# A decode layer on one core: w_gate loaded in two parts, residual sums moved between their matmuls, a smaller last load, and the store on another queue

## The chip, the cores and the metric

One core of a Trainium2 chip runs the kernel. The metric is the device time in microseconds (us) of one execution. A profile adds the kernel's *span*, which is 1.7 to 1.8 us shorter than the time that is measured from outside. Engines: PE is TensorE (PEld its weight loads), DVE is VectorE, ACT is ScalarE, SP is SyncE. SBUF is the on-chip memory that the loads fill, PSUM the one that TensorE writes its sums to.

## The reference

One token passes through an attention block and a gated MLP, batch 1, all in bf16:

```
x: [1, 1, 640]
h  = x + attention(layernorm(x))      # 32 heads, 4096 cached keys and values of 128 each, wq [640, 4096], wo [4096, 640]
g  = layernorm(h) @ w_gate            # [640, 1728]
u  = layernorm(h) @ w_up              # [640, 1728]
h2 = h + (gelu(g) * u) @ w_down       # [1728, 640]
```

Every weight and every cached row is used once. The bytes that must be read (84.2 MB; the kernel reads 84.3, since one load fetches rows that are already there) are therefore fixed, and the arithmetic on them is small.

## The kernel before

All big loads are issued by SyncE on one queue, in the order in which they are needed: wq, keys and values in turn, wo, and then the three MLP matrices. Three slots of SBUF hold keys, values and finally the MLP weights. The part that the change touches is the end. There hlnT is layernorm(h) as TensorE's operand, hX holds h for the residual sum, and hm is gelu(g) * u:

```python
    # issue order on SyncE, behind the last values and wo
    d_wd = [P.dma("sync", wd_sb[:, 12, :], B_w_down[1536:1664, :], free[1]),
            P.dma("sync", wd_sb[:, 13, :], B_w_down[1600:1728, :])]      # only its partitions 64 to 127 are used
    d_wg = P.dma("sync", wg_sb, B_w_gate[:, :].rearrange("(p c) n -> p c n", c=5), free[0])
    d_wu = [P.dma("sync", wu_sb[:, 0:3, :], wu_v[:, 0:3, :]),
            P.dma("sync", wu_sb[:, 3:5, :], wu_v[:, 3:5, :])]
    d_wd += [P.dma("sync", wd_d[:, 0:2, :, :], wd_v[:, 0:2, :, :]),      # "the bulk", 8 rows per partition
             P.dma("sync", wd_d[:, 2, 0:2, :], wd_v[:, 2, 0:2, :]),      # 2 rows
             P.dma("sync", wd_d[:, 2, 2:4, :], wd_v[:, 2, 2:4, :])]      # 2 rows, the last load
    # ...
    ga = T(glu(ps_g, wg_sb, range(5)), hl, d_wg)      # 70 matmuls: layernorm(h) @ w_gate
    T(resid, hx)                                      # residual sum: h into the output's PSUM
    T(glu(ps_u, wu_sb, range(3)), d_wu[0])            # 42 matmuls: w_up
    up = T(glu(ps_u, wu_sb, range(3, 5)), d_wu[1])    # 28
    # ... gelu(g) on DVE and ACT, then hm = gelu(g) * u
    T(down([12, 13], False), g9, d_wd[0], d_wd[1])    # 4 matmuls for each m
    T(down(range(8), False), d_wd[2])
    T(down([8, 9], False), d_wd[3])
    dn = T(down([10, 11], True), d_wd[4])
    # four copies PSUM -> out_row, two on DVE, two on ACT
    d_out = P.dma("sync", out[0, :, :], out_row[:, :], *os)
    P.op("sync", None, d_out)                         # wait for the store
```

The softmax here doesn't subtract the row's maximum and nothing guards it: scores larger than these inputs give would overflow.

Of the kernel before, what the change touches and what calls it, by code (L numbers as in the profile page):

```python
# [92 lines left out]
def bass_sequential_preLN__gqa_block_cached__glu_gated_geglu__decode_kernel(nc, A_x, A_k_cache, A_v_cache, A_wq, A_wo, B_x, B_w_gate, B_w_up, B_w_down, out):  # L93
# [11 lines left out]
    out_row = sb("out_row", [1, D], BF16)  # L105
# [29 lines left out]
    ps_g, ps_u = bank[0], bank[1]  # L135
# [11 lines left out]
    P = Prog(nc)  # L147
    V = lambda fn, *d: P.op("vector", fn, *d)
    A = lambda fn, *d: P.op("scalar", fn, *d)
    T = lambda fn, *d: P.op("tensor", fn, *d)  # L150
# [66 lines left out]
    def layernorm(src, ev, out_fn):  # L217
        s2 = V(lambda e: e.tensor_mul(src[:, 5:10], src[:, 0:5], src[:, 0:5]), ev)
        m = T(lambda e: e.matmul(ps_s[:, 16:26], mean_f[:, :], src[:, 0:10], start=True, stop=True), s2, c_mean)
        l1 = V(lambda e: e.reduce_sum(ln[:, 0:2], ps_s[:, 16:26].rearrange("p (a c) -> p a c", a=2), axis=AX.X), m)  # L220
        l2 = V(lambda e: e.scalar_tensor_tensor(out=ln[:, 2:3], in0=ln[:, 0:1], scalar=ln[:, 0:1],  # L221
                                                in1=ln[:, 1:2], op0=ALU.mult, op1=ALU.subtract), l1)
        l3 = A(lambda e: e.activation(ln[:, 3:4], ln[:, 2:3], ACTF.Ln, bias=eps_t[:, 0:1], scale=-1.0), l2, c_eps)  # L223
        l4 = A(lambda e: e.activation(ln[:, 4:5], ln[:, 3:4], ACTF.Exp, bias=zero_t[:, 0:1], scale=-0.5), l3)
        return V(out_fn, l4)
# [117 lines left out]
    for G in range(NG):  # L343
# [6 lines left out]
        if G == 4:  # L350
# [11 lines left out]
    free = [consumed[len(order) - NSLOT + i] for i in range(1, 3)]  # L362
    wg_sb = sl[0][:, 0:5 * DF].rearrange("p (c n) -> p c n", c=5)
# [3 lines left out]
    wd_v = B_w_down[0:1536, :].rearrange("(a p r) n -> p a r n", a=3, r=4)  # L367
    wd_d = wd_sb[:, 0:12, :].rearrange("p (a r) n -> p a r n", a=3)
    d_wd = [P.dma("sync", wd_sb[:, 12, :], B_w_down[1536:1664, :], free[1]),
            P.dma("sync", wd_sb[:, 13, :], B_w_down[1600:1728, :])]  # L370
    d_wg = P.dma("sync", wg_sb, B_w_gate[:, :].rearrange("(p c) n -> p c n", c=5), free[0])
    d_wu = [P.dma("sync", wu_sb[:, 0:3, :], wu_v[:, 0:3, :]),
            P.dma("sync", wu_sb[:, 3:5, :], wu_v[:, 3:5, :])]
    d_wd += [P.dma("sync", wd_d[:, 0:2, :, :], wd_v[:, 0:2, :, :]),
             P.dma("sync", wd_d[:, 2, 0:2, :], wd_v[:, 2, 0:2, :]),
             P.dma("sync", wd_d[:, 2, 2:4, :], wd_v[:, 2, 2:4, :])]

    V(lambda e: e.memset(ps_g[0:64, 13:14], 0.0), reds[31])
    V(lambda e: e.memset(ps_u[0:64, 13:14], 0.0), reds[31])
# [4 lines left out]
    hl = layernorm(hT, h, lambda e: e.tensor_scalar(  # L384
        hlnT[:, :], hT[:, 0:5], ln[:, 0:1], ln[:, 4:5], ALU.subtract, ALU.mult))
# [4 lines left out]
    def glu(ps, w, cs):  # L390
        def fn(e):
            for c in cs:
                for m in range(14):
                    ws = w[:, c, 512 * (m // 4) + m % 4:512 * (m // 4) + 512:4] if m < 12 else \
                        w[:, c, 128 * m:min(128 * m + 128, DF)]
                    i = e.matmul(ps[0 if m < 13 else 64:128, m:m + 1], ws, hlnT[:, c:c + 1],  # L396
                                 start=(c == 0 and m == 0), stop=(c == 4), skip_group_check=True)
            return i
        return fn
    ga = T(glu(ps_g, wg_sb, range(5)), hl, d_wg)  # L400


    def resid(e):
# [2 lines left out]
                         hX[:, 32 * q:32 * q + 32, :].rearrange("p a c -> p (a c)"), start=True, stop=False)  # L406
        return i
    T(resid, hx)
    T(glu(ps_u, wu_sb, range(3)), d_wu[0])
    up = T(glu(ps_u, wu_sb, range(3, 5)), d_wu[1])  # L410
    g1 = V(lambda e: e.tensor_copy(g_t[:, :], ps_g[:, 0:14]), ga)
# [9 lines left out]
    def down(ms, last):  # L421
        def fn(e):
            for m in ms:
                k = slice(0 if m < 13 else 64, 128)
                for q in range(4):
                    i = e.matmul(ps_d[32 * q:32 * q + 1, 0:160], hm[k, m:m + 1], wd_sb[k, m, 160 * q:160 * q + 160],  # L426
                                 start=False, stop=(last and m == ms[-1]))
            return i
        return fn
    T(down([12, 13], False), g9, d_wd[0], d_wd[1])  # L430
    T(down(range(8), False), d_wd[2])
    T(down([8, 9], False), d_wd[3])
    dn = T(down([10, 11], True), d_wd[4])
    os = [V(lambda e, q=q: e.tensor_copy(out_row[0:1, 160 * q:160 * q + 160], ps_d[32 * q:32 * q + 1, 0:160]), dn)  # L434
          for q in range(2)]
    os += [A(lambda e, q=q: e.copy(out_row[0:1, 160 * q:160 * q + 160], ps_d[32 * q:32 * q + 1, 0:160]), dn)
           for q in range(2, 4)]
    d_out = P.dma("sync", out[0, :, :], out_row[:, :], *os)
    P.op("sync", None, d_out)

    with nc.Block() as block:  # L441
        P.emit(block)
# [28 lines left out]
```

## Time and profile before

| | before |
|---|---|
| time, median of 3 runs | 205.82 us (205.62 to 205.85) |
| span of the profiled run | 204.0 us |
| SyncE's load queue, share of the 16 DMA engines' span | 97.0% |
| mean rate | 414 GB/s |
| last landing of a load | 201.30 us |
| from the last landing to the end of the span | 2.74 us |

Part 3 of the page of the kernel before, with packets, MB and the share of 16 engines' span for each DMA queue:

```profile
q1 hardware_dynamic: 4306, 84.32, 97.0%
q8 instruction: 8, 0.13, 0.3%
q14 instruction: 3, 0.02, 0.0%
q10 hardware_dynamic: 2, 0.00, 0.0%
```

The load queue is busy nearly all the time. The first thing to establish is therefore whether a change reaches the length of this stream, or the short piece behind it. On this reading nothing else can move the end.

The timeline of the kernel before, its last stage: start, duration, engine, line, operation, out<-in, count, and in brackets the idle time before it and what ended it. Lines that the argument doesn't need are left out, here and below.

```profile
191.54 3.35 PE L396 MATMUL bank<-hlnT,slot 128*128 128x1 bf16 x70 [3.22 <-DMA slot<-in_B_w_gate_dram]
195.48 3.38 PE L396 MATMUL bank<-hlnT,slot 128*128 128x1 bf16 x70
198.96 0.17 DVE L419 TENSOR_TENSOR hm<-gu,bank 128x14 bf16<-128x14 f32 x1 [2.20 <-PE bank L396]
199.19 0.32 PEld L426 LDWEIGHTS bank<-slot,hm 128*1 128x1 bf16 x8 [0.42 <-DVE hm L419]
199.78 1.16 PEld L426 LDWEIGHTS bank<-slot,hm 128*1 128x1 bf16 x40 [0.28 <-DMA slot<-in_B_w_down_dram]
201.34 0.10 PEld L426 LDWEIGHTS bank<-slot,hm 128*1 128x1 bf16 x8 [0.40 <-DMA slot<-in_B_w_down_dram]
201.83 0.60 ACT L436 CAST out_row<-bank 1x160 bf16<-1x160 f32 x2 [5.75 <-PE bank L426]
201.83 0.66 DVE L434 CAST out_row<-bank 1x160 bf16<-1x160 f32 x2 [2.70 <-PE bank L426]
202.52 0.32 SPq L51 DMA_DIRECT2D out_dram<-out_row  x1
```

Gate's 70 matmuls wait 3.22 us for their load. w_up's 70 have no wait: they run behind gate and the residual sum. hm is ready at 199.13 (198.96 + 0.17), and from there TensorE waits twice more for w_down: 0.28 us for the bulk and 0.40 us for the last load. Everything after 201.34 stands behind the last landing.

One row of the table of stretches of the kernel before (stretch, its length, busy time and count of PE, PEld, DVE, ACT and POOL, granted clock, DMA share, GB/s) shows the clock that TensorE has in this stage:

```profile
195.50:198.80 3.30, 3.30 (x74) 3.14 (x70) 0.79 (x5) 0.31 (x1) 0.00 (x0) 0.50 0.96 383
```

So TensorE is slow here, with a granted clock of 0.50, and busy all through the stretch. It still has to wait for the loads afterwards.

### The profile page before, as it was taken

To read this page: it belongs to the slowest core of one execution; us is meant where nothing else is said; L and a number is where in the kernel's file an instruction comes from. 1 tells how busy PE (TensorE), PEld (TensorE's weight loads), DVE (VectorE), ACT (ScalarE), POOL (GpSimd) and SP (SyncE) were. 2 spreads that over 40 slices of the span, in tenths; PEclk is the share of its full clock that TensorE was granted. 3 is DMA by queue.
4 is the path that set the end of the run, shared out by engine and by line. 5 is a ranking of instruction groups with operands and counts; after the bars stand their busy time and mean duration, and the time that the engine had idled before them with its cause. 6 is when DMAs were issued, how large, how long until landed. Compare 5 with 4: busy or idle time off the path is not lost.

```text
span 204.0 us, 2507 instructions
## 1 busy us (share of the span) xinstructions
PE 121.1 (59%) x1009; PEld 58.9 (29%) x1009; DVE 100.9 (49%) x104; ACT 61.1 (30%) x273; POOL 4.1 (2%) x12
## 2 busy tenths in 40 slices
PE   1007049567667808690977297637834787467494
PEld 1003013122222503250324032312411244267482
DVE  3100187799279327924791677287608760101221
ACT  2100103626706610670156035503630363100101
POOL 8000000000000000000000000000000000000000
PEclk9999757978969975998599859988995899965555
DMA  7999999999999999999999999999999999999991
GB/s 249 434 442 411 411 488 430 418 411 442 430 430 424 418 427 463 424 419 418 443 450 424 421 424 438 443 430 418 424 434 450 389 440 435 413 409 425 415 393 55
DMA packets 4319, 84.47 MB, mean 414 GB/s; under 512 B 466, under 2 KB 724, under 8 KB 1492
## 3 DMA queue, kind: packets, MB, share of 16 engines
q1 hardware_dynamic: 4306, 84.32, 97.0%
q8 instruction: 8, 0.13, 0.3%
q14 instruction: 3, 0.02, 0.0%
q10 hardware_dynamic: 2, 0.00, 0.0%
HBM read 84.31 MB, written 0.00 MB: 413 GB/s over the span
## 4 chain that ended last, share of the span: by engine, by line
DMA 64%; PE 14%; DVE 14%; SPq 4%; issue 3%; DVEq 0%
DMA slot<-in_A_k_cache_dram 43%; DVE prod L252 12%; DMA slot<-in_A_v_cache_dram 11%; DMA slot<-in_B_w_down_dram 10%; PE bank L260 10%; SPq L51 4%; PE bank L289 3%; DVE sc L267 2%; PE bank L298 1%; PE bank L426 0%; DVEq L441 0%; DVE out_row L434 0%; PE bank L309 0%; DVE RT L308 0%
## 5 line engine op out<-in xcount | busy, mean ns | idle before, releaser
L260 PE MATMUL bank<-prod,id_b 128*128 128x512 bf16 x256 | 75.8, 457 | 53.6 <-DVE prod L252 53.5
L252 DVE TENSOR_TENSOR prod<-slot,qb 128x4096 bf16<-128x4096 bf16 x32 | 72.4, 2284 | 31.6 <-DMA slot<-in_A_k_cache_dram 31.6
L271 ACT ACTIVATE p_bd<-sc,zero_t 32x32 bf16<-32x32 f32 x128 | 46.4, 363 | 89.0 <-DVE sc L267 87.8
L260 PEld LDWEIGHTS bank<-prod,id_b 128*128 128x128 bf16 x256 | 27.1, 114 | 102.5 <-DVE prod L252 66.1
L267 DVE TENSOR_REDUCE sc<-bank 128x32 f32<-128x512 f32 x32 | 22.0, 688 | 21.5 <-PE bank L260 21.4
L271 ACT ACTIVATION_READ_ACCUMULATOR p_bd<-sc,zero_t 32x1 f32 x128 | 23.5, 184 | 0.0
L289 PE MATMUL bank<-slot,p_bd 128*16 128x512 bf16 x256 | 17.2, 379 | 0.6 <-DMA slot<-in_A_v_cache_dram 0.6
L289 PEld LDWEIGHTS bank<-slot,p_bd 128*16 128x16 bf16 x256 | 9.4, 89 | 4.8 <-DMA slot<-in_A_v_cache_dram 1.1
L238 PE MATMUL bank<-arena,xlnB 128*32 128x512 bf16 x40 | 4.1, 586 | 11.3 <-DMA arena<-in_A_wq_dram 11.3
L298 PE MATMUL bank<-po_sb,hs 128*16 128x128 f32 x64 | 8.4, 274 | 1.1 <-ACT po_sb L293 1.1
L327 PE MATMUL bank<-aP,arena 128*128 128x1 bf16 x160 | 6.7, 178 | 3.8 <-DMA arena<-in_A_wo_dram 3.8
L396 PE MATMUL bank<-hlnT,slot 128*128 128x1 bf16 (+1 forms) x140 | 6.7, 176 | 3.2 <-DMA slot<-in_B_w_gate_dram 3.2
L327 PEld LDWEIGHTS bank<-aP,arena 128*128 128x128 bf16 x160 | 6.6, 131 | 4.0 <-DMA arena<-in_A_wo_dram 2.6
L396 PEld LDWEIGHTS bank<-hlnT,slot 128*128 128x128 bf16 (+1 forms) x140 | 6.3, 118 | 4.1 <-issue 3.8
L242 DVE CAST qb<-bank 128x512 bf16<-128x512 f32 x1 | 0.7, 692 | 13.8 <-PE bank L238 13.8
L293 ACT COPY po_sb<-bank 128x512 f32<-128x512 f32 x8 | 4.7, 586 | 7.6 <-PE bank L289 7.6
L298 PEld LDWEIGHTS bank<-po_sb,hs 128*16 128x16 f32 x64 | 5.5, 96 | 4.5 <-issue 2.1
L223 ACT ACTIVATE ln<-ln,eps_t 128x1 f32<-128x1 f32 x2 | 0.6, 294 | 17.0 <-DVE ln L221 17.0
L238 PEld LDWEIGHTS bank<-arena,xlnB 128*32 128x32 bf16 x40 | 1.6, 141 | 13.3 <-issue 13.3
L383 DVE TENSOR_TENSOR hT<-xx,bank 128x5 f32<-128x5 f32 x1 | 0.2, 161 | 10.3 <-PE bank L327 10.3
L243 ACT CAST qb<-bank 128x512 bf16<-128x512 f32 x1 | 0.6, 586 | 14.3 <-PE bank L238 14.3
L313 DVE TENSOR_SCALAR aT<-bank,rz 16x128 bf16<-16x128 f32 x2 | 0.7, 339 | 6.0 <-PE bank L298 6.0
(59 smaller groups left out, 24.6 us busy)
## 6 DMA issues: line engine op xcount, KB each, us to landing
slot<-in_A_k_cache_dram SPq DMA_DIRECT2D x8, 4096.0 KB, 22.3
slot<-in_A_v_cache_dram SPq DMA_DIRECT2D x7, 4096.0 KB, 17.4
arena<-in_A_wq_dram SPq DMA_DIRECT2D x1, 5120.0 KB, 15.4
slot<-in_A_v_cache_dram SPq DMA_DIRECT2D x2, 2048.0 KB, 20.9
arena<-in_A_wo_dram SPq DMA_DIRECT2D x1, 2560.0 KB, 28.7
slot<-in_B_w_gate_dram SPq DMA_DIRECT2D x1, 2160.0 KB, 15.4
arena<-in_A_wo_dram SPq DMA_DIRECT2D x1, 1920.0 KB, 32.8
slot<-in_B_w_up_dram SPq DMA_DIRECT2D x1, 1296.0 KB, 18.0
```

Source lines behind the costliest of these rows:

```text
L51: ev = self.op(eng, lambda e: e.dma_start(out, in_), *deps, dma=True)
L238: i = e.matmul(ps_q[hf][32 * j:32 * j + 32, :], xlnB[:, c, :], wq_j[:, c, j, 4 * hf:4 * hf + 4, :], start=(c == 0), stop=(c == 4))
L242: qa = V(lambda e: e.tensor_copy(qb[:, 0:4, :].rearrange("p g d -> p (g d)"), ps_q[0][:, :]), qd)
L252: m = V(lambda e: e.tensor_tensor(out=prod[:, s % 4, :, :], in0=kt[:, 32 * u:32 * u + 32, :], in1=qb[:, G, :].unsqueeze(1).to_broadcast([1 ...
L260: i = e.matmul(ps_f[s % 2][:, :], id_b[:, :], prod[:, s % 4, :, 16 * b:16 * b + 16], start=(b == 0), stop=(b == 7))
L267: reds[s] = V(lambda e: e.reduce_sum(sc[:, s % 4, :], ps_f[s % 2][:, :].rearrange("p (g d) -> p g d", d=16), axis=AX.X), folds[s], exps.ge ...
L271: x = A(lambda e, j=j: e.activation(p_bd[32 * j:32 * j + 32, G % 2, 32 * (s % 4):32 * (s % 4) + 32, j], sc[32 * j:32 * j + 32, s % 4, :], ...
L289: i = e.matmul(po[a:a + 16, :], p_bd[:, G % 2, 4 * b:4 * b + 4, :].rearrange("p g j -> p (g j)"), vt[:, 4 * b:4 * b + 4, :], start=(b < 4) ...
L293: evs[G] = A(lambda e: e.copy(po_sb[:, G % 2, :], po[:, :]), pvs[G], hds.get(G - 2))
L298: i = e.matmul(ps_a[0:16, 128 * (G // 4):128 * (G // 4) + 128], hs[:, r, 12 - 4 * g:28 - 4 * g], po_sb[:, G % 2, 128 * r:128 * r + 128], s ...
L327: r = e.matmul(ps_p[:, c:c + 1], wo_sb[:, t, i, c::5], aP[:, t, i:i + 1], start=(t == 0 and c == 0 and i == 0), stop=(t == 1 and i == 15), ...
L396: i = e.matmul(ps[0 if m < 13 else 64:128, m:m + 1], ws, hlnT[:, c:c + 1], start=(c == 0 and m == 0), stop=(c == 4), skip_group_check=True)
```

## The change

Its intent: let gate start as soon as three fifths of w_gate are there; use the wait for the rest for the residual sums; leave as little work as possible behind the last load; and take the store to the queue of the engine that does the last copies.

```diff
-    d_wg = P.dma("sync", wg_sb, B_w_gate[:, :].rearrange("(p c) n -> p c n", c=5), free[0])
+    wg_v = B_w_gate[:, :].rearrange("(p c) n -> p c n", c=5)
+    d_wg = [P.dma("sync", wg_sb[:, 0:3, :], wg_v[:, 0:3, :], free[0]),
+            P.dma("sync", wg_sb[:, 3:5, :], wg_v[:, 3:5, :])]
     ...
-             P.dma("sync", wd_d[:, 2, 0:2, :], wd_v[:, 2, 0:2, :]),
-             P.dma("sync", wd_d[:, 2, 2:4, :], wd_v[:, 2, 2:4, :])]
+             P.dma("sync", wd_d[:, 2, 0:3, :], wd_v[:, 2, 0:3, :]),
+             P.dma("sync", wd_d[:, 2, 3:4, :], wd_v[:, 2, 3:4, :])]
     ...
-    ga = T(glu(ps_g, wg_sb, range(5)), hl, d_wg)
+    T(glu(ps_g, wg_sb, range(3)), hl, d_wg[0])
     ...
     T(resid, hx)
+    ga = T(glu(ps_g, wg_sb, range(3, 5)), d_wg[1])
     ...
-    T(down([8, 9], False), d_wd[3])
-    dn = T(down([10, 11], True), d_wd[4])
+    T(down([8, 9, 10], False), d_wd[3])
+    dn = T(down([11], True), d_wd[4])
     ...
-    d_out = P.dma("sync", out[0, :, :], out_row[:, :], *os)
-    P.op("sync", None, d_out)
+    d_out = P.dma("scalar", out[0, :, :], out_row[:, :], *os)
+    P.op("scalar", None, d_out)
```

## The prediction

> **What bounds the kernel.** The loads on SyncE's DMA queue. The table of DMA queues gives that queue 97.0% of the 16 engines' span, at a mean of 414 GB/s; the slices show DMA at nine tenths from the second to the next to last. The chain of waits is 64% DMA and ends: last w_down load (landing at 201.30), last matmul group 0.47, copies 0.66, the store, end at 204.0. TensorE is not the limit in the last stage, although the table of stretches grants it a clock of 0.5: hm is ready at 199.13, the first eight w_down matmuls start at 199.19, the next wait 0.28 for the load landing at 199.74, and the last eight 0.40 for the load landing at 201.30. So only the 2.7 us after the last landing, and the stream's length, can move the time.
>
> **The change, part by part.**
>
> 1. *w_gate in two loads.* Three fifths would land some 2 us (864 KB at about 413 GB/s) before 191.41, at about 189.3, so the first 42 gate matmuls can start when hlnT is ready (189.76), not at 191.54. Gate should end near 193.9 with the residual sums between, instead of 194.9. w_up's landings (194.50, 196.62) then gate w_up: hm ready near 198.2 instead of 199.13. But w_down's bulk lands at 199.74 whatever TensorE does. Slack grows (0.28 to about 1.3 us); the end doesn't move.
> 2. *Residual sums between* (0.71 us of TensorE): moved in slack, nothing.
> 3. *Stream.* Same bytes. w_gate's packets of 17280 B took 644 ns; they become 10368 and 6912 B, which w_up's already are, at 389 and 263 ns: 8 ns more for each of eight rows per engine, 0.06 us. The w_down tail, two 2560 B packets at 102 ns, becomes 3840 B (about 150, estimated) and 1280 B at 55: nothing. Last landing: +0 to +0.1 us.
> 4. *Last load halved.* Four matmuls after the last landing instead of eight. The second group of four starts only 0.09 us after the first, so 0.09 us is saved. The load before it lands 0.4 us later (about 200.9, was 200.51); its 12 matmuls take under 0.4 us, so just fit ahead of 201.3. At worst they delay the last four by 0.1.
> 5. *Store by ScalarE's queue.* The copies end at 202.49 and SyncE's issue starts at 202.52: no dead hop to remove. The issue took 0.32 us and landed 0.8 after it. ScalarE's only DMA issue (x, at the start) took 0.51 us, SyncE's first 0.38. [...] Expect -0.05 to +0.2 us.
>
> Sum: +0.06 - 0.09 + 0.05, nearly nothing. **Predicted 205.7 us, 8 in 10 between 204.9 and 206.4; faster by over 2%: 0.01, within 2%: 0.98, slower: 0.01.**
>
> **What would show it.** In the timeline after: gate starts near 189.8, hm ready about 1 us earlier; a longer wait of w_down's matmuls for the 199.7 landing; last landing within 0.3 us of 201.3; the last matmuls about 0.09 us shorter; the store issued by ScalarE for at least 0.3 us right after 202.4. DMA share and GB/s as before.
>
> **What would make it wrong.** A stream at another rate (1% is 2 us) from the other packet sizes; issues that block SyncE longer (two took 1.40 and 3.32 us) with one more load queued; a store clearly slower or faster from ScalarE; or the 12 matmuls running into the last four.

The sum: +0.06 - 0.09 + 0.05 = +0.02 us.

## The result, and the profile after

The kernel after takes 205.55 us (median of 5 runs, 205.35 to 205.84). The kernel before takes 205.62 us over its 5 runs (205.38 to 205.85). The ratio is 0.9997, with a 95% interval of 0.9984 to 1.0011: the same.

The DMA queues of the kernel after (packets, MB, share):

```profile
q1 hardware_dynamic: 4448, 84.31, 97.1%
q8 instruction: 8, 0.13, 0.3%
```

There are 142 packets more, and the bytes and the share are as good as unchanged (84.31 MB against 84.32, 97.1% against 97.0%). The timeline of the kernel after, same stage and columns as before:

```profile
189.72 2.06 PE L398 MATMUL bank<-hlnT,slot 128*128 128x1 bf16 x42 [1.50 <-DVE hlnT L386]
191.70 0.71 PE L407 MATMUL bank<-hX,ones_f 128*1 128x160 f32 x8
192.35 1.38 PE L398 MATMUL bank<-hlnT,slot 128*128 128x1 bf16 x28
194.48 3.49 PE L398 MATMUL bank<-hlnT,slot 128*128 128x1 bf16 x70 [0.75 <-DMA slot<-in_B_w_up_dram]
198.07 0.17 DVE L422 TENSOR_TENSOR hm<-gu,bank 128x14 bf16<-128x14 f32 x1 [2.48 <-PE bank L398]
198.30 0.32 PEld L429 LDWEIGHTS bank<-slot,hm 128*1 128x1 bf16 x8 [0.42 <-DVE hm L422]
199.70 0.89 PEld L429 LDWEIGHTS bank<-slot,hm 128*1 128x1 bf16 x32 [1.09 <-DMA slot<-in_B_w_down_dram]
200.87 0.23 PEld L429 LDWEIGHTS bank<-slot,hm 128*1 128x1 bf16 x12 [0.28 <-DMA slot<-in_B_w_down_dram]
201.27 0.09 PEld L429 LDWEIGHTS bank<-slot,hm 128*1 128x1 bf16 x4 [0.17 <-DMA slot<-in_B_w_down_dram]
201.63 0.59 ACT L439 CAST out_row<-bank 1x160 bf16<-1x160 f32 x2 [6.72 <-PE bank L429]
201.63 0.66 DVE L437 CAST out_row<-bank 1x160 bf16<-1x160 f32 x2 [3.38 <-PE bank L429]
202.32 0.23 ACTq L51 DMA_DIRECT2D out_dram<-out_row  x1
```

Gate now starts 1.8 us earlier (189.72 against 191.54), and what ends its wait is hlnT, not the load. hm is ready at 198.24 instead of 199.13. That gain turns into waits at once: 0.75 us for w_up where there was none, and 1.09 us for the bulk of w_down where there was 0.28. The matmuls of the bulk start at 199.70 instead of 199.78. Behind the last landing (201.23) the first copy starts after 0.40 us instead of 0.53, and the span ends after 2.60 us instead of 2.74.

### The profile page after: what moved, and what is told of

It reads as the page before. It is cut to its first block, busy times and chain, and to the rows that moved or that the text cites. A ratio compares the mean times of both kernels' runs of the same rounds, so it can differ in the third digit from the quotient of the medians.

```text
span 203.8 us, 2508 instructions
## 1 busy us (share of the span) xinstructions
PE 120.8 (59%) x1009; PEld 58.7 (29%) x1009; DVE 100.8 (49%) x104; ACT 61.1 (30%) x273; POOL 4.1 (2%) x12
## 3 DMA queue, kind: packets, MB, share of 16 engines
q1 hardware_dynamic: 4448, 84.31, 97.1%
HBM read 84.31 MB, written 0.00 MB: 414 GB/s over the span
## 4 chain that ended last, share of the span: by engine, by line
DMA 65%; PE 15%; DVE 15%; issue 2%; SPq 2%; DVEq 0%
DMA slot<-in_A_k_cache_dram 44%; DVE prod L252 12%; DMA slot<-in_A_v_cache_dram 11%; DMA slot<-in_B_w_down_dram 11%; PE bank L260 9%; PE bank L289 3%; DVE sc L267 2%; SPq L51 2%; PE bank L298 1%; PE bank L429 1%; DVEq L444 0%; DVE out_row L437 0%; PE bank L309 0%; DVE RT L308 0%
```

## The experiments

**The theories.** A: the end is set by the last landing of the load stream and by what follows it; the gate part only makes slack on TensorE; the end gains about 0.1 us from the smaller last load. B: TensorE at half clock does lie on the path, and another part of the change ate what gate gained. C: one of the parts of the tail alone made the whole gain of the tail. D: the gate part made no slack that can be used at all.

Three columns of the table below come from the landing records of each profile. Each of these loads runs on 16 DMA engines, and each engine reports its part: there are 16 reports for a load. *Mean landing* and *last landing* are taken over the 16 reports of the last load. *Tail* is the span minus the last landing. The experiments ran in three groups, each on one chip together with the kernel before: e1, e3, e4 and e5 (before 205.60 us, median of 11 runs), e2, e6, e7 and e8 (205.65), and e9 to e12 (205.51).

| run | median us | ratio to before (95%) | mean landing | last landing | tail |
|---|---|---|---|---|---|
| before | 205.62 | | 199.91 | 201.30 | 2.74 |
| after | 205.55 | 0.9997 (0.9984 to 1.0011) | 199.92 | 201.23 | 2.60 |
| e1_gate_only | 205.75 | 1.0000 (0.9985 to 1.0015) | 199.94 | 200.85 | 2.74 |
| e2_down_only | 205.43 | 0.9990 (0.9974 to 1.0006) | 199.83 | 201.40 | 2.64 |
| e3_store_only | 205.57 | 0.9995 (0.9977 to 1.0013) | 199.88 | 201.26 | 2.72 |
| e4_before_more_pe | 206.62 | 1.0051 (1.0031 to 1.0070) | 200.10 | 202.25 | 3.49 |
| e5_after_more_pe | 205.24 | 0.9982 (0.9966 to 0.9999) | 199.71 | 200.69 | 2.60 |
| e6_half_rows | 206.02 | 1.0009 (0.9985 to 1.0033) | 199.94 | 200.81 | 2.59 |
| e7_wide_copy | 205.86 | 1.0007 (0.9990 to 1.0025) | 199.79 | 201.34 | 2.84 |
| e8_wide_half | 206.35 | 1.0027 (1.0010 to 1.0044) | 200.33 | 201.52 | 2.88 |
| e9_more_fetches | 206.73 | 1.0063 (1.0045 to 1.0081) | 200.51 | 202.36 | 2.59 |
| e10_after_again | 205.30 | 0.9992 (0.9974 to 1.0010) | 199.78 | 200.71 | 2.60 |
| e11_wide_copy_sync | 205.57 | 1.0005 (0.9988 to 1.0021) | 199.93 | 201.04 | 2.80 |
| e12_after_more_pe_again | 205.84 | 1.0010 (0.9990 to 1.0029) | 199.94 | 201.36 | 2.60 |

Read the columns before the single runs. The tail repeats to 0.01 us among runs with the same tail (2.59 or 2.60 in after, e5, e6, e9, e10 and e12). The last landing does not: in after and e10, which are the same kernel, it is 201.23 and 200.71. A gain of 0.14 us in the tail is therefore clear in the traces and lost in the times. All kernels gave right results.

### e1, e2, e3: one part of the change at a time

e1 is the kernel before with the w_gate lines of the diff above and the order gate, residual sum, gate.

> Kernel before with only the w_gate split and the residual sums between its sums. Theory A (the end is set by the last landing and what follows it): gate matmuls start near 189.8, hm is ready near 198.2 instead of 199.13, the wait of the w_down matmuls for the 199.7 landing grows from 0.28 to about 1.1 us, and the tail from the last landing to the end stays 2.74 us; time within 0.1 us of before. Rival B (TensorE's work at half clock is on the path at the end, and other parts of the change ate its gain): faster by 0.5 to 1 us.

The timeline of e1:

```profile
189.30 2.05 PE L398 MATMUL bank<-hlnT,slot 128*128 128x1 bf16 x42 [1.50 <-DVE hlnT L386]
194.07 3.48 PE L398 MATMUL bank<-hlnT,slot 128*128 128x1 bf16 x70 [0.76 <-DMA slot<-in_B_w_up_dram]
197.66 0.17 DVE L422 TENSOR_TENSOR hm<-gu,bank 128x14 bf16<-128x14 f32 x1 [2.48 <-PE bank L398]
199.32 1.16 PEld L429 LDWEIGHTS bank<-slot,hm 128*1 128x1 bf16 x40 [1.12 <-DMA slot<-in_B_w_down_dram]
200.89 0.10 PEld L429 LDWEIGHTS bank<-slot,hm 128*1 128x1 bf16 x8 [0.41 <-DMA slot<-in_B_w_down_dram]
```

hm stands 3.02 us ahead of the last landing (200.85 - 197.83), where it was 2.17 us in before (201.30 - 199.13). The wait for the bulk grew from 0.28 to 1.12 us. The tail is 2.74 us, as in before, and so is the time (ratio 1.0000). This is theory A; theory B wanted 0.5 to 1 us.

e2 is the kernel before with the three-and-one split of the last w_down rows only.

> Kernel before with only the last load of w_down cut to one row per partition. Theory A: one group of four matmuls fewer after the last landing, so from landing to first copy 0.40 to 0.45 us instead of 0.53, tail 2.62 to 2.66 instead of 2.74; time 0.1 us under before. Rival C: tail unchanged at 2.74, since the load before now lands 0.4 us later and its 12 matmuls run into the last ones (hm comes as late as before).

The tail is 2.64 us and the first copy starts 0.43 us behind the last landing: 0.10 us gained, as theory A expected, although hm came late here (199.27). Timeline of e2:

```profile
199.93 0.90 PEld L426 LDWEIGHTS bank<-slot,hm 128*1 128x1 bf16 x32 [0.29 <-DMA slot<-in_B_w_down_dram]
201.07 0.46 PEld L426 LDWEIGHTS bank<-slot,hm 128*1 128x1 bf16 x16 [0.25 <-DMA slot<-in_B_w_down_dram]
201.83 0.60 ACT L436 CAST out_row<-bank 1x160 bf16<-1x160 f32 x2 [5.61 <-PE bank L426]
```

The second line merges the 12 weight loads for the load of 201.03 with the 4 for the last one (201.40). In the single records the 12 start from 201.07 to 201.17 and the last of their matmuls at 201.31; the last four weight loads start at 201.44, 0.04 us behind the landing, as they do in before (201.34 behind 201.30). So the larger load before the last fits ahead of it, just as the prediction had worked out.

e3 is the kernel before with the store on ScalarE's queue only.

> Kernel before with only the store moved to ScalarE's queue. Theory A: issue to landing about 0.03 to 0.1 us shorter, copies to issue unchanged at 0.03; tail from the last landing 2.70 to 2.75 us. Rival C (the store alone gave what the change gained): tail 2.60 us. Time: within 0.1 us of before for both, so the tail of the trace decides.

The timeline of e3:

```profile
202.48 0.23 ACTq L51 DMA_DIRECT2D out_dram<-out_row  x1
```

The tail is 2.72 us. The issue took 0.23 us, and issue to landing 1.09 us (202.48 to 203.57), against 0.32 and 1.13 on SyncE. The copies still end 0.03 us ahead of the issue. So the store gave 0.02 us, and theory C falls for the store; e2 has most of the gain. The three parts add up: 0.00 + 0.10 + 0.02 = 0.12 us, and all together gave 0.14.

### e4 and e5: is the slack real?

The same block of needless matmuls goes into both kernels, between gate and w_up:

```diff
+    def more(e):
+        for c in range(3):
+            for m in range(14):
+                i = e.matmul(ps_s[:, 64:65], wg_sb[:, c, 0:128], hlnT[:, c:c + 1], start=True, stop=True)
+        return i
+    T(more)
     T(glu(ps_u, wu_sb, range(3)), d_wu[0])
```

> Kernel before with 42 needless matmuls (about 2 us at the half clock) between gate and w_up, written to unused PSUM columns. Theory A: TensorE's slack at the end of before is 0.28 us up to the 199.74 landing and at most 0.7 us in all, so hm comes 2.0 us later (about 201.1) and the run is 1.0 to 1.5 us slower. Rival D (TensorE has much slack here anyway and the gate split bought none that can be used): within 0.2 us of before.

> Kernel after with the same 42 needless matmuls at the same place. Theory A: w_up's sums waited 0.75 us for their load and hm came 1.1 us ahead of the 199.7 landing, so most of the 2.0 us disappears: hm near 199.4, end within 0.3 us of before; about 1 us faster than the before with the same matmuls. Rival D: no difference between the two with added matmuls.

In e4 (timeline):

```profile
196.42 1.28 PE L412 MATMUL bank<-hlnT,slot 128*128 128x1 bf16 x42
197.56 3.36 PE L396 MATMUL bank<-hlnT,slot 128*128 128x1 bf16 x70
201.03 0.17 DVE L425 TENSOR_TENSOR hm<-gu,bank 128x14 bf16<-128x14 f32 x1 [3.31 <-PE bank L396]
201.25 1.89 PEld L432 LDWEIGHTS bank<-slot,hm 128*1 128x1 bf16 x56 [0.42 <-DVE hm L425]
```

In e5 (timeline):

```profile
193.13 1.28 PE L415 MATMUL bank<-hlnT,slot 128*128 128x1 bf16 x42
194.27 3.36 PE L398 MATMUL bank<-hlnT,slot 128*128 128x1 bf16 x70
197.74 0.17 DVE L428 TENSOR_TENSOR hm<-gu,bank 128x14 bf16<-128x14 f32 x1 [2.67 <-PE bank L398]
199.15 0.89 PEld L435 LDWEIGHTS bank<-slot,hm 128*1 128x1 bf16 x32 [0.87 <-DMA slot<-in_B_w_down_dram]
```

In e4 all 56 w_down weight loads run in one block behind hm, with no wait for a load: TensorE has become the limit, and the tail is 3.49 us. In e5 most of the block disappears in the wait for w_up (it landed at 193.86, and its matmuls start 0.41 us later), the w_down matmuls still wait 0.87 us for the bulk, and the tail is 2.60 us. The medians, from one chip, are 206.62 and 205.24 us, where before has 205.60: the added work costs before 1.02 us, and after with it is no slower than before. (The kernel after was not run in this group. Beside it, in e12, the same kernel was 0.54 us slower, with the same tail of 2.60 us and a last landing 0.65 us later; that difference is taken up below.) So the gate part does what it was made for. There is just nothing in this kernel that uses the room. Theory D falls.

Two things in my expectation were off. The 42 matmuls took 1.14 us from their start to that of the next, not 2 (196.42 to 197.56 and 193.13 to 194.27), because I had costed them like gate's (70 in 3.35 us). At clock 0.50 gate's matmuls start every 33 ns, but the starts around its one 64-column tile (m = 13) lie about 96 and 145 ns apart in the groups of 14. These 42, all of one shape with contiguous weights, started every 27 ns. That the change of shape makes the gaps is the obvious reading; no run here isolates it. And hm of e4 is 2.07 us later than in before only because w_gate's landing was 0.94 us later in this profile too (192.35 against 191.41). That is why the size of the slack is not read from these times.

### e6, e7, e8, e11: two attempts at a faster kernel

Theory A says where to look: fewer bytes, or a shorter tail. e6 is the kernel after, but it loads only the 64 partitions of the w_down tail that are used, 80 KB less:

```diff
-            P.dma("sync", wd_sb[:, 13, :], B_w_down[1600:1728, :])]
+            P.dma("sync", wd_sb[64:128, 13, :], B_w_down[1664:1728, :])]
```

> Kernel after, but the w_down load of which only partitions 64 to 127 are used loads only these: 80 KB less of 84.3 MB. Theory A (the stream's length sets the end): last landing 0.2 us earlier, time 0.2 us under after. Rival B: TensorE sets the end, nothing gained.

The expectation failed. The last landing of one profile is no evidence (200.81 here, 200.71 in e10 without this edit). The mean landing is steadier: from the last values' load to the last load of the kernel it takes 28.53 to 28.56 us in after, e1, e5, e7, e9, e10, e11 and e12, but 28.81 and 28.82 us in e6 and e8. Loading 80 KB less made the stream 0.26 us *longer*. At the mean rate of 414 GB/s it should have been 0.20 us shorter, by my estimate. The 1280 B packets in this stretch (170 to 190 us) have a median of 55 ns in both, but a 90th percentile of 60 and a longest of 68 ns in after, and 69 and 148 ns in e6. The landing records show that the neighbouring loads lose. Counted from the last values' load, the mean landing of the last wo load, two places ahead of the edited one, is already 0.12 us later in e6 and 0.17 in e8 than in after; at the first w_gate load it is 0.25 and 0.28, and from the mean landing of the load before it to its own the edited load takes 0.36 us (0.37 in e8) instead of 0.43, for half of the bytes. Why the load is hardly cheaper, and why the neighbours lose, no run here isolates.

e7 is the kernel after with one copy per engine over 64 partitions, of which four rows of the 128 are the result, and a store from those four:

```diff
-    os = [V(lambda e, q=q: e.tensor_copy(out_row[0:1, 160 * q:160 * q + 160], ps_d[32 * q:32 * q + 1, 0:160]), dn)
-          for q in range(2)]
-    os += [A(lambda e, q=q: e.copy(...), dn) for q in range(2, 4)]
-    d_out = P.dma("scalar", out[0, :, :], out_row[:, :], *os)
+    os = [V(lambda e: e.tensor_copy(out_all[0:64, :], ps_d[0:64, 0:160]), dn),
+          A(lambda e: e.copy(out_all[64:128, :], ps_d[64:128, 0:160]), dn)]
+    d_out = P.dma("scalar", out[0, :, :].rearrange("a (q n) -> (a q) n", q=4), out_all[0:128:32, :], *os)
```

> Kernel after with the output copied out of PSUM by one instruction per engine (64 partitions x 160, four of the 128 rows are wanted) instead of two of one row each, and stored from four partitions. Theory A (the tail after the last landing is on the path one for one): copies take 0.31 us instead of 0.66, end 0.35 us earlier if the store from four partitions takes as long as from one; time 0.25 to 0.4 us under after. If the four-row store lands later, this is what is lost.

The timeline of e7:

```profile
201.74 0.32 DVE L437 CAST out_all<-bank 64x160 bf16<-64x160 f32 x1 [3.39 <-PE bank L429]
202.11 0.61 ACTq L51 DMA_DIRECT2D out_dram<-out_all  x1
```

The copies did fall from 0.66 to 0.32 us. But the issue of the store rose from 0.23 to 0.61 us, and issue to landing from 1.10 to 1.66 us (202.11 to 203.77), with four rows of 320 B instead of one of 1280 B. The tail is 2.84 us instead of 2.60. More was lost than won.

e8 is e6 and e7 together:

> Both of the last two on top of the kernel after. Theory A: the gains add up, 0.45 to 0.6 us under after, about 205.0 us on a chip that gives before 205.6.

The expectation failed with its two parts. It is the slowest of the four (e6, e7, e8 and e11), with both losses: 28.82 us of stream and a tail of 2.88. e11 asks whether the four rows or ScalarE make the store slow; it is e7 with "sync" in place of "scalar" for the store.

> The wide copy with the four-row store issued by SyncE instead of ScalarE. There ScalarE's issue took 0.61 us against 0.23 for one row, and issue to landing 1.66 against 1.10. If the four rows are what costs, the same here (1.6 us or more from issue to landing, tail 2.8 us); if it was ScalarE, issue about 0.32 and landing about 1.15, tail 2.3 us and the time 0.3 us under after.

The timeline of e11:

```profile
201.44 0.32 DVE L437 CAST out_all<-bank 64x160 bf16<-64x160 f32 x1 [3.39 <-PE bank L429]
201.81 0.63 SPq L51 DMA_DIRECT2D out_dram<-out_all  x1
```

From SyncE the issue took 0.63 us and issue to landing 1.65 us (201.81 to 203.46), tail 2.80. So it is the four rows and not the engine. Most of the 0.5 us that four rows need more than one is the issue (0.61 against 0.23 from ScalarE, 0.63 against 0.32 from SyncE); from its end to the landing it is 1.05 against 0.87 and 1.01 against 0.82. Why is open.

### e9, e10, e12: what scatters the last landing

Every profile shows the 16 engines finishing the last load at different times: 1.8 to 3.5 us lie between the first and the last. The gap hardly changes over many loads in a row (1.81 to 1.84 us for those complete from 55.6 to 143.1), so I took the engines' shares of a load to be equal and looked for when the gap opens. These are the gaps between the first and the last of the 16 reports for successive loads of the kernel before, with the starts of the 16384 B packets of queue q8 ("instruction") beside them:

```
load complete at    45.3   55.6  ...  143.1   153.6  ...  201.3
gap, us              1.24   1.83       1.84    2.65        2.52
instruction packets at 47.6, 74.3, 113.1, 149.1, 174.5, 187.9, 196.7 and 200.9, each about 1.0 us
```

A gap of 1.26 us is there from the first load of all, before any of these packets, and stays unexplained. The rest opens in two steps, and a packet falls into each of them (with one of 8192 B on q14, at 49.8, in the first). The other packets left the gap nearly as it was. The records do not name the engine, so that a step lies on the very engine that such a packet (a *fetch* below, after the queue's label) ran on is inferred. To test what the packets cost the loads, e9 makes TensorE's program longer by 768 one-column matmuls, in gaps where TensorE waits for VectorE (54.0 us in all at the fold matmuls of the kernel after). That a longer program brings more of the packets was my estimate; the result below shows it:

```diff
         folds[s] = T(fold, m, c_idb, reds.get(s - 2))
+        def filler(e):
+            for _ in range(24):
+                i = e.matmul(ps_s[:, 64:65], id_b[:, :], ones_b[:, 0:1], start=True, stop=True)
+            return i
+        T(filler, c_onesb)
```

> Kernel after with 24 needless one-column matmuls behind each of the 32 fold groups, where TensorE waits for VectorE: 768 matmuls, 1536 instructions more. Theory E (the last landing is late because single DMA engines also fetch instructions, 16384 B in about 1.0 us each, 8 of them in the span, and each step of the spread between first and last landing follows one): about six more such packets, the mean landing of the last load 0.2 to 0.3 us later, spread between its first and last engine 2.5 us or more, time 0.2 to 1.0 us over after. Rival (fetches do not matter): last landing 200.7 to 201.5 and time as after.

> The kernel after, unchanged, as the control of this call. Both theories: as before within 0.2 us; last landing between 200.7 and 201.5, tail from it 2.60 us.

> The kernel after with the 42 needless matmuls, again, now beside the kernel after. If the lead of 0.3 us that it had was chance (last landing 200.69 in its profile[...]), it is within 0.2 us of after here. If filling TensorE there really helps, it leads by 0.3 us again.

The DMA queues of e9:

```profile
q1 hardware_dynamic: 4448, 84.31, 96.7%
q8 instruction: 14, 0.23, 0.4%
```

There are 14 packets instead of 8. The first engine to finish the last load does so at 198.85 us, as in after and e10 (198.79 and 198.86): the stream as a whole was not held up, which fits engines that fetched nothing and lost nothing. The mean landing is 0.73 us later than in e10 (200.51 against 199.78), the last landing 1.65 us later, and the median 1.43 us (206.73 against 205.30). The tail is unchanged at 2.59. The direction was as expected, the size over it: my expectation of 0.2 to 0.3 us for the mean and at most 1 us for the time was too low. Part of the larger number is the luck of the profiles: against after the mean is 0.59 us later and the last landing 1.13. Six packets at 1.05 us over 16 engines would be 0.39 us of mean (an estimate from the packets' durations), so a fetch costs more than its packet.

How much more, the landing records of all 14 profiles tell. From one 4096 KB load of keys or values to the next the mean landing advances by 9.70 to 9.72 us when no instruction packet starts between the two, and by 9.80 to 9.82 us when one of 16384 B alone does (in e12 one at the border of two loads counts for the earlier). So each fetch holds the mean back by about 0.10 us, which is 1.6 us of one engine for a packet of about 1.0 us, and six of them by 0.6 us: the 0.59 against after. Why it is more than the packet is open. One load is an exception: the one complete near 65 us takes up to 0.34 us more although, outside e9, no such packet falls on it. In e5, e6 and e10, where SyncE issued it before 50.4 us, it takes 0.00 to 0.04 more; in the other eleven profiles, issued from 50.5 us on, 0.14 to 0.34. These three are also the profiles with the earliest last landings (200.69 to 200.81). That the late issue is the cause is likely, but not tested; it accounts for most of what e9 lost to e10 beyond the six fetches.

e10 is the kernel after again: 205.30 us, ratio 0.9992. e12 is e5 again. In its own group e5 had seemed 0.36 us faster than before; beside the kernel after, the same kernel was 0.54 us slower than it (205.84 against 205.30), with a last landing of 201.36 instead of 200.69. That is outside the 0.2 us that I had expected for chance, on the other side. The lead of e5 did not repeat, and I take it for chance: the two profiles of this one kernel differ in the load near 65 us (0.00 and 0.18 us more) and in the last landing, not in the tail. No version tried beats both kernels by an amount that these runs can show.

## Why the prediction was right

1. **Bound by the stream and its tail: right.** e1 brought hm 0.85 us further ahead of the last landing and the end did not move. e4 put more than a microsecond in and the end did move, because before's slack is small; e5 shows that after has room for it.
2. **Gate in two loads: right, each number close.** Start 189.72 (forecast 189.8), end of gate 193.73 (193.9), hm 198.24 (198.2), wait for the bulk 1.09 us (about 1.3).
3. **Stream: right.** Mean landings take 28.51 us from the last values to the last load in before, e2 and e3 (28.54 in e4), and 28.55 in after and e1: the split of w_gate costs some 0.04 us (forecast 0.06 from the packets' durations).
4. **Last load: right.** 0.09 us forecast; e2 measured 0.10.
5. **Store: right that it is nothing, wrong in sign within its range.** I had leaned to +0.05 us from ScalarE's first issue (0.51 us, at the start of the kernel). The issue at the end took 0.23 us there (the forecast was at least 0.3), against SyncE's 0.32, and e3 gained 0.02. I had expected nothing to save; 0.09 us of issue was there, of which 0.04 reached the landing (issue to landing 1.09 us in e3 against 1.13 in before).

The sum was -0.09 + 0.06 + 0.05 = +0.02 us, and the traces give about -0.14 in the tail and +0.04 in the stream. What I had not seen is that the last landing itself scatters by half a microsecond between runs of one kernel. These times could not have shown a change of this size; only the tails of the traces do. So that 205.7 us came within 0.15 us of the median says little: the forecast that nothing moves is what was tested.

## What to carry to other kernels

When loads bound a kernel, cut its end at the last landing. Here the work ahead of it was slack however busy its engine looked, up to the point where it ran past the landing (e4 went past it), and only the bytes, the engine time of the DMA packets and the tail behind the landing counted. Test slack by adding the same work to both kernels: one that has gained room shows it at once, although its own time has not moved. Compare small changes by the pieces of the trace that repeat (here the tail to 0.01 us, the time between two mean landings to 0.03), not by times that scatter by half a microsecond, and repeat a lead near the edge of its interval beside its control before believing it.
